# One tile for the first decays, another order of the opening, and two queues for the last stores

## The chip, the cores and the metric

One Trainium2 chip, one core of it. The metric is device time in microseconds (us). Engines are named as in the profile: PE (TensorE, matrix products, with its weight loads PEld), DVE (VectorE), ACT (ScalarE), POOL (GpSimd), SP (SyncE, which issues DMAs). ACT can issue DMAs too; an issue occupies the issuing engine's sequencer, and the transfer then runs by itself. Each engine takes its instructions in the order in which the program was written.

## The reference

Two stages. The first is a scan over a sequence with decays `a`, for 4 sequences, 8 heads, 768 positions; in chunks it reads:

```
log_a = log(clip(a, 1e-6, 1))
cum   = cumsum(log_a in the chunk)
M     = (C @ B.T) * exp(cum_i - cum_j) * (i >= j)
y     = M @ x + (C @ state) * exp(cum)
state = exp(sum log_a) * state + sum_j B_j x_j exp(cum_end - cum_j)
```

Its output, as 3072 tokens of 256 features, goes to the second, a mixture of four experts with gates `p`:

```
p   = probs / (sum(probs) + 1e-9)
out = sum_e p[:, e] * (relu(x @ w1[e]) @ w2[e])
```

All is float32: w1 is 4 x 256 x 1024, w2 4 x 1024 x 256.

## The kernel before

A token chunk is 128 positions; two halves of 64 of every chunk column make a pair p, and 12 pairs cover the sequences. The experts' products run in four blocks of three pairs over 256-wide blocks of features. Sums and differences of weights and of tokens are formed on DVE and POOL so that fewer products are needed (the tables `G` and `B`), and their results are combined on DVE.

The program has two parts. The **opening** (L560 to L786) is written out by hand in the order in which the engines are to take it, and computes the first pair. Everything behind it goes through a **planner** (class `Plan`, L71): every piece of work is added with an engine (or two to choose from), an estimated duration, what it reads and writes, and sometimes a due time. PE's pieces stand in a fixed list `line`; `Plan.run` (L181) walks through a model of time, starting each engine at a time given at the end (`START` for PE, `now` and offsets for the others, L1614), and chooses for the other engines what comes next and which buffer it takes. The order found is the order of the program. Absolute times occur in it as thresholds (`OPENING` 80, `SURE` 100, `BUSY` 200).

What the steps of the prediction touch, in the opening:

- **Loads.** `load_heads` (L445) brings B and C of the four sequences for one chunk column, in two halves of two sequences, both on SP (L569, L579). `load_a` (L573) brings raw decays of one chunk column: 8 KB for each half `s` of the sequences, into every 32nd partition of a tile `a_q[s]` that has been set to zero, one on SP and one on ACT (L577). `a_q2` (L566) are such tiles for the next chunk column, loaded on SP (L589). ACT issues the load of the gates' probabilities first (L570), and two loads of tokens before it loads its table (L582). `load_w1` and `load_w2` follow on SP.
- **Decays.** `ready` (L616) clips a tile on DVE. The clip's upper bound is `own` (L608): 1 in the partitions that hold data, 0 elsewhere. `spread` (L662) sends the decays to the 64 partitions of the half `s` of four banks by a product with ones: first all four row groups `q` for `s` = 0, then for `s` = 1. `scan` (L506) multiplies up the running products from a bank on DVE, one for each `q`.
- **Scores.** `mask` (L486) selects heads of C on ACT; `score` (L492) makes the products C B of one half `s` in four banks `seven`; `masked` (L687) multiplies them by the scans' result on DVE, `aside` (L682) does so for one `q` through ACT and POOL.
- **Gates.** POOL sums the probabilities (L625 to L628), DVE takes the reciprocal (L629), POOL multiplies (L636). `turn_gates` (L644) transposes them on PE into the upper halves of the first two banks `seven[:2]` (called `As`), and ACT copies them out. `spread_gate` (L654) sends them to all partitions through a bank of `seven[2:]` (called `ys`), and ACT copies that.
- **Logs.** `turn_logs` (L700) takes logarithms on ACT, transposes them on PE through a bank (before: `ys[0]`) and ACT copies them; `sum_logs` (L706) makes the sums, which go to DRAM for the later pairs.
- `inner` (L529, products at L532) multiplies the masked scores by the tokens. `idle` (L691) is a product of ones whose result nobody reads; it keeps PE occupied.

PE's order before is at L740 to L782: idle products, `spread`, idle, first half of the scores, turns of the gates, second half of the scores, turns of the logs, spread of the gate, `inner`, the second spread, sums of the logs, the state, the third spread; then the planned `line` with products at L987 (function `product`).

The **end** is `last` (L1378): the results of the last block are turned by PE, copied from their bank by ACT or DVE in turns (L1409, L1461) and stored by `send` (L1395). It is called seven times and issues two DMAs each time, one for each half of the partitions, both on SP.

Of the kernel before, what the change touches and what calls it, by code (L numbers as in the profile page):

```python
# [8 lines left out]
FP32 = mybir.dt.float32  # L9
AF = mybir.ActivationFunctionType  # L10
ALU = mybir.AluOpType

P = 128
# [346 lines left out]
def kernel(  # L360
# [83 lines left out]

    def load_heads(k, bct, zs=slice(0, NSEQ)):  # L445
        src = xbc.rearrange("(z k) r w -> k r z w", k=NC)
        nc.sync.dma_start(out=bct[:, zs], in_=src[k][:, zs, OBT:])

# [43 lines left out]
    def score(p, ctm, bct, banks, half=0, only=None):  # L492
        e = p % 2
        for c in range(2):
            lo = FB * half + P * c
            for s in range(2) if only is None else (only,):
                for r in range(NQ):
                    k, to = slice(32 * r, 32 * r + 32), slice(HALF * s, HALF * s + HALF)
                    nc.tensor.matmul(  # L499
                        out=banks[r][to, lo:lo + P].rearrange("p (t i) -> p t i", t=NT),  # L500
                        lhsT=bct[k, 2 * s + c, 0, HALF * e:HALF * e + HALF],
                        rhs=ctm[k, :, 2 * s + c],
                        start=(c == 0 and not half), stop=True, tile_position=(32 * r, HALF * s),
                        skip_group_check=True)
# [54 lines left out]

    a_q = [homes["V"][-1 - s].rearrange("p c (t x) -> p c t x", t=NT) for s in range(2)]  # L560

# [3 lines left out]
    xt, bct = homes["xt"], homes["bct"]  # L565
    a_q2 = [homes["V"][-4 - s].rearrange("p c (t x) -> p c t x", t=NT) for s in range(2)]  # L566
    nc.vector.memset(a_q[0], 0.0)
    nc.gpsimd.memset(a_q[1], 0.0)
    load_heads(0, bct[0], slice(0, 2))  # L569
    nc.scalar.dma_start(out=pr, in_=probs)  # L570
    a_rows = a.rearrange("(s c k) (q t) x -> k s q c (t x)", s=2, c=2, t=NT)

    def load_a(k, s, a_q, queue):  # L573
        queue.dma_start(
            out=a_q[s].rearrange("(q r) c t x -> q r c (t x)", q=NQ)[:, 0], in_=a_rows[k, s])
# [33 lines left out]
    nc.vector.reduce_sum(  # L609
        own.unsqueeze(2), ident.rearrange("p (q r) -> p r q", r=32)[:, 0:1],  # L610
        axis=mybir.AxisListType.X)

    def clip(engine, v, top=1.0):
        engine.tensor_scalar(out=v, in0=v, scalar1=1e-6, scalar2=top, op0=ALU.max, op1=ALU.min)

    def ready(v, e):  # L616
        v = v.rearrange("p c t (e i) -> p (c t) e i", e=2)[:, :, e]
        clip(nc.vector, v, own)
        nc.vector.memset(v[:, :, 0:1], 0.0)

    for s in range(2):
        ready(a_q[s], 0)

# [4 lines left out]
    nc.gpsimd.tensor_scalar_add(total_p, total_p, 1e-9)  # L628
    nc.vector.reciprocal(total_p, total_p)  # L629
    upto = const.tile([P, P], FP32)  # L630
# [4 lines left out]
    nc.gpsimd.memset(upto[:HALF, HALF:], 0.0)  # L635
    nc.gpsimd.tensor_mul(  # L636
        pc.rearrange("p z e k -> p z k e"), pr.rearrange("p (z k) e -> p z k e", z=NSEQ),
        total_p.rearrange("p (z k) e -> p z k e", z=NSEQ).to_broadcast([P, NSEQ, NC, E]))

    BANK = homes["bank"]  # L640
# [21 lines left out]
    def spread(a_q, e, banks, half, order=range(NQ)):  # L662
        for s in range(2):
            for q in order:
                k = slice(32 * q, 32 * q + 32)
                nc.tensor.matmul(  # L666
                    out=banks[q][HALF * s:HALF * s + HALF, FB * half:FB * half + FB].rearrange(
                        "p (x i) -> p x i", x=4),
                    lhsT=one[k].to_broadcast([32, HALF]),
                    rhs=a_q[s].rearrange("p c t x -> p (c t) x")[k, :, HALF * e:HALF * e + HALF],  # L670
                    start=True, stop=True, tile_position=(32 * q, HALF * s), skip_group_check=True)
# [19 lines left out]
    def idle(bank, lo, to):  # L691
        nc.tensor.matmul(
            out=bank.rearrange("p (w s) -> p w s", s=P)[:, lo:to], lhsT=one.to_broadcast([P, P]),
            rhs=one.unsqueeze(1).to_broadcast([P, to - lo, P]), start=True, stop=True,
            skip_group_check=True)
# [44 lines left out]
    idle(BANK[6], 0, 4)  # L740
    idle(BANK[7], 0, 3)
    spread(a_q, 0, four, 0, ORDER)
    idle(BANK[7], 0, 1)
    for s in range(2):
        mask(0, ctm[0], bct[0], slice(2 * s, 2 * s + 2))
    score(0, ctm[0], bct[0], seven, 0, 0)
    for q in ORDER:
        scan(0, q, MT[0], four[q], 0)
    turn_gates(As)
    score(0, ctm[0], bct[0], seven, 0, 1)  # L750
    clip(nc.gpsimd, a_sb)
# [7 lines left out]
    for s in range(2):  # L759
        ready(a_q[s], 1)  # L760
    for c in range(2):
# [13 lines left out]
    for s in range(2):  # L775
        ready(a_q2[s], 0)
    spread(a_q, 1, four, 1, ORDER)
# [14 lines left out]
    B512, B256 = {"DVE": D512, "POOL": 1.3}, {"DVE": D256, "POOL": .72}  # L792
    now, START = 10.2, 11.6

# [5 lines left out]
    def dma(fn, n=1, kb=256, **kw):  # L800
        return plan.add({"SP": ISSUE * n}, fn, lag=LANDING + kb / 190, kb=kb, pieces=n, **kw)
# [576 lines left out]
    def last(k, groups):  # L1378
# [16 lines left out]
        def send(d, n, r, to):  # L1395
            dma(lambda e: [nc.sync.dma_start(
                out=dst[d, 3 * k + n, c][:, to],
                in_=r.t[HALF * c:HALF * c + HALF, 0, to.start * P:to.stop * P].rearrange(
                    "p (s m) -> p s m", m=P)) for c in range(2)],
                2, kb=64 * (to.stop - to.start), reads=[r])  # L1400

# [269 lines left out]
```

## Time and profile before

| | us |
|---|---|
| median of 3 runs | 617.71 |
| lowest, highest | 615.79, 618.04 |
| the profiled execution | 618.47 |
| its span, first to last instruction | 616.8 |
| granted clock of PE over the span | 0.995 |

| engine | busy us | share of the span |
|---|---|---|
| PE | 603.9 | 98% |
| PEld | 517.8 | 84% |
| DVE | 497.9 | 81% |
| ACT | 276.9 | 45% |
| POOL | 139.3 | 23% |

The profile is of one execution; its times count from the start of the span. A row of its timeline gives the start and the duration in us (of several instructions of one kind together, from the first to the last), the engine, the line of the kernel, the operation, what it writes and reads by the names of the tiles, the shapes, and how many. In brackets stands how long the engine had been idle before, and what ended that. A queue (SPq, ACTq) shows the issuing of DMAs, not their transfer. Matrix products are pipelined, so that rows of PE overlap.

### The profile page before, as it was taken

How to read it: one execution, taken by the hardware profiler on the slowest of the kernel's cores; microseconds unless marked ns; L12 is line 12 of the kernel's file. 1: busy time of each engine (PE TensorE's matmuls, PEld its weight loads, DVE VectorE, ACT ScalarE, POOL GpSimd, SP SyncE). 2: the span in 40 equal slices, each digit the busy share in tenths (PEclk: the TensorE clock that was granted, in tenths of full speed). 3: DMA queues.
4: the chain of work that ended last, by engine and by line, in shares of the span. 5: the costliest groups of instructions: out<-in, count | busy, mean ns of one | idle time of the engine just before them, and what ended most of it. 6: DMA issues, size and time to landing. Idle time of an engine off the chain costs nothing.

```text
span 616.8 us, 12247 instructions
## 1 busy us (share of the span) xinstructions
PE 603.9 (98%) x4526; PEld 517.8 (84%) x4526; DVE 497.9 (81%) x858; ACT 276.9 (45%) x624; POOL 139.3 (23%) x147
## 2 busy tenths in 40 slices
PE   7999999999999999999999999999999999999995
PEld 4777888888888888888888888878888888888884
DVE  4769999999999995786988987486876989485783
ACT  3337557575442626765243343434444242524430
POOL 5572555655610000367401000000000000000000
PEclk9999999999999999999999999999999999999999
DMA  7477677778733329773432416863342323963002
GB/s 206 127 212 211 206 215 244 238 229 292 236 98 113 84 34 324 202 255 137 136 95 69 118 31 172 288 188 95 86 128 70 103 63 62 356 209 94 1 0 53
DMA packets 99856, 93.78 MB, mean 152 GB/s; under 512 B 33500, under 2 KB 69052, under 8 KB 99796
## 3 DMA queue, kind: packets, MB, share of 16 engines
q1 hardware_dynamic: 99272, 92.70, 49.3%
q8 instruction: 36, 0.59, 0.4%
q10 hardware_dynamic: 524, 0.30, 0.2%
q14 instruction: 24, 0.20, 0.1%
HBM read 72.79 MB, written 20.17 MB: 151 GB/s over the span
## 4 chain that ended last, share of the span: by engine, by line
PE 95%; DVE 2%; issue 1%; DMA 1%; ACT 0%; SPq 0%; DVEq 0%
PE bank L987 89%; PE bank L532 2%; PE bank L499 1%; PE bank L920 1%; PE bank L541 1%; DVE v L1022 1%; PE bank L666 1%; DVE MT L520 1%; DMA pr<-in_probs_dram 0%; DVE v L1014 0%; PE bank L1456 0%; DVE bank L1145 0%; PE bank L1393 0%; DVE v L1536 0%; DMA v<-in_a_dram 0%
## 5 line engine op out<-in xcount | busy, mean ns | idle before, releaser
L987 PE MATMUL bank<-v,w 128*128 128x256 f32 x1876 | 435.2, 380 | 1.2 <-DVE bank L1145 0.7
L987 PEld LDWEIGHTS bank<-v,w 128*128 128x128 f32 x1876 | 354.7, 190 | 52.3 <-DVE bank L1145 1.6
L1014 DVE TENSOR_TENSOR v<-v,v 128x512 f32<-128x512 f32 x238 | 177.1, 766 | 1.7
L987 PE MATMUL bank<-Y,w 128*128 128x256 f32 x692 | 177.1, 380 | 0.0
L1287 ACT COPY v<-bank 128x512 f32<-128x512 f32 x120 | 70.3, 586 | 202.7 <-PE bank L987 199.1
L987 PEld LDWEIGHTS bank<-Y,w 128*128 128x128 f32 x692 | 130.6, 190 | 19.4 <-ACT v L996 0.9
L1022 DVE SCALAR_TENSOR_TENSOR v<-bank,gate 128x512 f32<-128x512 f32 x162 | 111.1, 686 | 40.2 <-PE bank L987 35.5
L1047 POOL TENSOR_TENSOR w<-w,w 128x512 f32<-128x512 f32 (+1 forms) x84 | 94.1, 1132 | 104.6 <-DVE v L1022 32.7
L1001 ACT COPY bank<-v 128x512 f32<-128x512 f32 x141 | 81.7, 593 | 20.7 <-DVE v L1022 14.5
L1145 DVE TENSOR_TENSOR bank<-bank,v 128x512 f32<-128x512 f32 x92 | 62.6, 693 | 33.7 <-PE bank L987 23.3
L996 ACT COPY v<-bank 128x512 f32<-128x512 f32 x111 | 65.1, 587 | 53.0 <-PE bank L987 45.3
L515 ACT ACTIVATE MT<-ab,neg 128x64 f32<-128x64 f32 x144 | 37.4, 338 | 0.0
L1014 DVE TENSOR_TENSOR v<-bank,v 128x512 f32<-128x512 f32 x30 | 20.6, 685 | 9.3 <-PE bank L987 6.4
L1323 DVE TENSOR_TENSOR v<-v,v 128x256 f32<-128x256 f32 x65 | 24.5, 416 | 1.0 <-ACT v L1287 0.7
L1022 DVE SCALAR_TENSOR_TENSOR v<-v,gate 128x512 f32<-128x512 f32 x30 | 24.1, 804 | 0.4
L882 POOL TENSOR_TENSOR cts<-ctm,dec 128x512 f32<-128x512 f32 x11 | 14.0, 1270 | 36.0 <-DVE Y L1117 24.2
L939 ACT COPY v<-bank 64x256 f32<-64x256 f32 (+1 forms) x33 | 12.3, 373 | 19.6 <-PE bank L541 12.4
L1014 POOL TENSOR_TENSOR v<-v,v 128x512 f32<-128x512 f32 x12 | 15.2, 1271 | 16.0 <-DVE v L1014 9.7
L689 DVE TENSOR_TENSOR MT<-bank,MT 128x256 f32<-128x256 f32 x47 | 16.6, 412 | 1.6 <-PE bank L499 1.6
L520 DVE TENSOR_TENSOR MT<-MT,bound 128x512 f32<-128x512 f32 x18 | 15.8, 891 | 0.0
L489 ACT ACTIVATE ctm<-bct,tmask 128x256 f32<-128x256 f32 (+1 forms) x26 | 11.4, 485 | 7.0 <-DMA bct<-in_xbc_dram 6.9
L532 PEld LDWEIGHTS bank<-MT,xt 64*32 64x32 f32 x768 | 10.1, 109 | 2.9 <-issue 2.0
(95 smaller groups left out, 188.7 us busy)
## 6 DMA issues: line engine op xcount, KB each, us to landing
w<-w_d SPq DMA_DIRECT2D x128, 256.0 KB
w<-in_w_dram SPq DMA_DIRECT2D x72, 256.0 KB
w_d<-w SPq DMA_DIRECT2D x64, 256.0 KB
gate<-p_d SPq DMA_DIRECT2D x15, 384.0 KB
ab<-cum_d SPq DMA_DIRECT2D x36, 128.0 KB
xt<-in_xbc_dram SPq DMA_DIRECT2D x46, 96.0 KB
bct<-in_xbc_dram SPq DMA_DIRECT2D x5, 512.0 KB
out_dram<-v SPq DMA_DIRECT2D x144, 16.0 KB
```

Source lines behind the costliest of these rows:

```text
L515: nc.scalar.activation(out=MT[:, q, c, t], in_=ab[:, c, h], func=AF.Exp, bias=neg[:, e, t, i:i + 1])
L520: nc.vector.tensor_tensor(out=v, in0=v, in1=bound.unsqueeze(1).to_broadcast([P, 4 * n, HALF]), op=ALU.min)
L532: nc.tensor.matmul(out=y[to:to + 32], lhsT=xt[k, c, h:h + D], rhs=MT[k, q, c, t], start=start, stop=True, tile_position=(HALF * s, to), sk ...
L987: nc.tensor.matmul(out=o, lhsT=w[:, j], rhs=x if half is None else x[:, j], start=(start and j == 0), stop=(j == 1), skip_group_check=True)
L996: act(.5, lambda e: nc.scalar.copy(out=flat(v), in_=bank.t), reads=[bank], writes=[v])
L1001: act(.54 if to - lo > FB else .32, lambda e: nc.scalar.copy(out=bank.t[:, lo:to], in_=flat(v)[:, lo:to]), reads=[v], writes=[bank])
L1014: plan.add(engines, lambda e: (on(e).tensor_add if sign > 0 else on(e).tensor_sub)(flat(v), whole(x), whole(y)), reads=[x, y], writes=[v], ...
L1022: dve(D512, lambda e: nc.vector.scalar_tensor_tensor(out=h.t, in0=whole(x).rearrange("p (j m) -> p j m", j=JJ), scalar=0.0, in1=g.t[:, 2 * ...
L1047: (on(e).tensor_add if sign > 0 else on(e).tensor_sub)(out, x, y)
L1145: dve(D512, lambda e: (nc.vector.tensor_add if sign > 0 else nc.vector.tensor_sub)(to.t, bank.t, whole(x)), reads=[x, bank], writes=[to])
L1287: act(.5, lambda e: nc.scalar.copy(out=flat(v), in_=bank.t), reads=[bank], writes=[v], hold=HOLD)
L1323: plan.add(engines, lambda e: (on(e).tensor_add if sign > 0 else on(e).tensor_sub)(o[1](), x[1](), y[1]()), reads=[v for v in vs if v is n ...
```

## The change

- The tiles `a_q[0]` and `a_q[1]` become one tile, `a_q`, with the half `s` in every 32nd partition counted from `s`; so do those of `a_q2`. `ready` clips the whole tile in one instruction with an upper bound of 1. `own` now has two columns, a mask of the rows of each half, and takes the place of the ones in `spread`, which goes through the halves inside each row group.
- The loads of the decays come before the heads; the second half of the heads is issued by ACT. Two w1 loads come before those of `a_q2`.
- The reciprocal and the multiplication of the gates move behind the first scan; the gates are turned before both halves of the scores, which follow each other. The logs are turned behind `inner`, through `As[1]`. One idle product is cut from 384 to 256 columns, one of 128 is added before the masks, one of 128 ahead of `inner`.
- The planner's `now` and `START` become 0.6 smaller, and two tiles of V fewer are marked as used by the opening.
- `send` puts its two DMAs into the plan one by one, the first on SP, the second on ACT.

```diff
-    def load_heads(k, bct, zs=slice(0, NSEQ)):
+    def load_heads(k, bct, zs=slice(0, NSEQ), queue=nc.sync):
...
-    a_q = [homes["V"][-1 - s].rearrange("p c (t x) -> p c t x", t=NT) for s in range(2)]
+    a_q, a_q2 = (homes["V"][-i].rearrange("p c (t x) -> p c t x", t=NT) for i in (1, 4))
...
-    nc.vector.memset(a_q[0], 0.0)
-    nc.gpsimd.memset(a_q[1], 0.0)
-    load_heads(0, bct[0], slice(0, 2))
+    nc.vector.memset(a_q[:, 0], 0.0)
+    nc.gpsimd.memset(a_q[:, 1], 0.0)
     nc.scalar.dma_start(out=pr, in_=probs)
...
-            out=a_q[s].rearrange("(q r) c t x -> q r c (t x)", q=NQ)[:, 0], in_=a_rows[k, s])
+            out=a_q.rearrange("(q r) c t x -> q r c (t x)", q=NQ)[:, s], in_=a_rows[k, s])
 
     for s, queue in enumerate((nc.sync, nc.scalar)):
         load_a(0, s, a_q, queue)
-    load_heads(0, bct[0], slice(2, 4))
+    load_heads(0, bct[0], slice(0, 2))
+    load_heads(0, bct[0], slice(2, 4), nc.scalar)
...
-    for s in range(2):
-        nc.vector.memset(a_q2[s], 0.0)
+    nc.vector.memset(a_q2, 0.0)
+    for fb in range(2):
+        load_w1(fb, homes["W"][fb])
     for s in range(2):
         load_a(1, s, a_q2, nc.sync)
-    for fb in range(4):
+    for fb in range(2, 4):
...
-    own = const.tile([P, 1], FP32)
+    own = const.tile([P, 2, 1], FP32)
...
-        clip(nc.vector, v, own)
+        clip(nc.vector, v)
...
-        for s in range(2):
-            for q in order:
+        for q in order:
+            for s in range(2):
...
-                    lhsT=one[k].to_broadcast([32, HALF]),
+                    lhsT=own[k, s].to_broadcast([32, HALF]),
...
-    idle(BANK[7], 0, 3)
+    idle(BANK[7], 0, 2)
     spread(a_q, 0, four, 0, ORDER)
+    idle(BANK[7], 0, 1)
     idle(BANK[7], 0, 1)
     for s in range(2):
         mask(0, ctm[0], bct[0], slice(2 * s, 2 * s + 2))
-    score(0, ctm[0], bct[0], seven, 0, 0)
-    for q in ORDER:
+    for i, q in enumerate(ORDER):
         scan(0, q, MT[0], four[q], 0)
+        if not i:
+            nc.vector.reciprocal(total_p, total_p)
+    nc.gpsimd.tensor_mul(
+        pc.rearrange("p z e k -> p z k e"), pr.rearrange("p (z k) e -> p z k e", z=NSEQ),
...
     turn_gates(As)
-    score(0, ctm[0], bct[0], seven, 0, 1)
+    for s in range(2):
+        score(0, ctm[0], bct[0], seven, 0, s)
...
-    turn_logs(ys[0])
     spread_gate(ys[1], homes["gate"][0])
-    for s in range(2):
-        ready(a_q[s], 1)
+    idle(four[0], 2, 3)
+    ready(a_q, 1)
...
+    turn_logs(As[1])
     for s, copy in enumerate((nc.scalar.copy, nc.vector.tensor_copy)):
...
-    now, START = 10.2, 11.6
+    now, START = 9.6, 11.0
...
-    for i in (0, NV - 5, NV - 4, NV - 2, NV - 1):
+    for i in (0, NV - 4, NV - 1):
...
         def send(d, n, r, to):
-            dma(lambda e: [nc.sync.dma_start(
-                out=dst[d, 3 * k + n, c][:, to],
...
-                2, kb=64 * (to.stop - to.start), reads=[r])
+            for c, (queue, on_) in enumerate(((nc.sync, "SP"), (nc.scalar, "ACT"))):
+                plan.add({on_: ISSUE}, lambda e, c=c, queue=queue: queue.dma_start(
...
+                        "p (s m) -> p s m", m=P)), lag=LANDING + .2, kb=32 * (to.stop - to.start),
+                    reads=[r])
```

More of the change, by code (lines that the diff above doesn't have):

```diff
@@ L443, in load_tokens @@
                 out=xt[HALF * s:HALF * s + HALF, c], in_=src[s, c, k, e][:, :OBT])
-    def load_heads(k, bct, zs=slice(0, NSEQ)):
+    def load_heads(k, bct, zs=slice(0, NSEQ), queue=nc.sync):
         src = xbc.rearrange("(z k) r w -> k r z w", k=NC)
-        nc.sync.dma_start(out=bct[:, zs], in_=src[k][:, zs, OBT:])
+        queue.dma_start(out=bct[:, zs], in_=src[k][:, zs, OBT:])
     def load_decays(p, ab):
@@ L607, with clip @@
                             op0=ALU.mult, op1=ALU.add)
-    own = const.tile([P, 1], FP32)
+    own = const.tile([P, 2, 1], FP32)
     nc.vector.reduce_sum(
[L610 to L614, printed above, removed]
+        own, ident.rearrange("p (q r) -> p r q", r=32)[:, 0:2], axis=mybir.AxisListType.X)
+    def clip(engine, v):
+        engine.tensor_scalar(out=v, in0=v, scalar1=1e-6, scalar2=1.0, op0=ALU.max, op1=ALU.min)
     def ready(v, e):
         v = v.rearrange("p c t (e i) -> p (c t) e i", e=2)[:, :, e]
-        clip(nc.vector, v, own)
+        clip(nc.vector, v)
         nc.vector.memset(v[:, :, 0:1], 0.0)
-    for s in range(2):
-        ready(a_q[s], 0)
+    ready(a_q, 0)
     pairs = const.tile([P, T // P, 2], FP32)
@@ L774 @@
              in_=ys[s][:, :FB].rearrange("p (c t i) -> p c t i", c=2, t=NT))
-    for s in range(2):
-        ready(a_q2[s], 0)
+    ready(a_q2, 0)
     spread(a_q, 1, four, 1, ORDER)
```

13 lines of the change are left out of this document (4 added, 9 removed).

## The prediction, made before the result was known

> **What bounds the kernel now.** First the page's chain by engine and the busy time of each engine over the planned middle, then the two ends in order of time.
>
> ```profile
> PE 95%; DVE 2%; issue 1%; DMA 1%; ACT 0%; SPq 0%; DVEq 0%
> ```
> ```profile
> 20.00:600.00 580.00, 578.76 (x4269) 500.77 (x4269) 483.62 (x812) 270.08 (x607) 129.99 (x119) 1.00 0.50 154
> 46.00:231.00 185.00, 184.48 (x1500) 158.36 (x1499) 180.86 (x298) 102.38 (x264) 73.06 (x63) 1.00 0.59 184
> ```
>
> The columns of the second fence are the stretch, its length, and the busy time of PE, PEld, DVE, ACT and POOL. The chain is PE's, and from 20 to 600 us PE is busy 578.76 of 580: it can win at most 1.2 us there. So the change can gain only ahead of the first weight product and behind the last matmul. In 46 to 231 us DVE is at 180.86 of 185 too; this is where the middle could lose.
>
> The opening in order of time (start, busy, instruction, what ended the idle time before it), on PE, then DVE, ACT, POOL and SP's queue:
>
> ```profile
> 0.84 3.33 PE L692 MATMUL bank<-const-float32-1.0 128*128 128x512 f32 x4 [0.84 <-PEq L1663]
> 6.11 1.57 PE L666 MATMUL bank<-v,const-float32-1.0 32*64 32x256 f32 x16 [1.94 <-DVE v L619]
> ...
> 8.33 1.13 PE L499 MATMUL bank<-ctm,bct 32*64 32x128 f32 x16
> 9.39 1.03 PE L646 MATMUL bank<-ident,pc 128*24 128x128 f32 x4
> 10.44 1.08 PE L499 MATMUL bank<-ctm,bct 32*64 32x128 f32 x16
> 12.31 0.39 PE L703 MATMUL bank<-ident,cum 96*128 96x96 f32 x2 [0.78 <-ACT cum L701]
> 12.62 0.69 PE L655 MATMUL bank<-v,ident 24*128 24x256 f32 x2
> ...
> 13.78 2.33 PE L532 MATMUL bank<-MT,xt 64*32 64x64 f32 x62 [0.24 <-ACT gate L659]
> 16.03 1.16 PE L666 MATMUL bank<-v,const-float32-1.0 32*64 32x256 f32 x16
> ...
> 19.94 2.43 PE L987 MATMUL bank<-v,w 128*128 128x256 f32 x10
> ```
> ```profile
> 5.57 0.75 DVE L614 TENSOR_SCALAR v<-v,own 128x256 f32<-128x256 f32 x2 [2.45 <-DMA v<-in_a_dram]
> ...
> 6.36 0.29 DVE L629 RECIPROCAL total_p<-total_p 128x24 f32<-128x24 f32 x1
> ...
> 7.66 2.44 DVE L507 TENSOR_TENSOR_SCAN MT<-bank,identr 128x256 f32<-128x256 f32 x4 [1.01 <-PE bank L666]
> 11.68 1.09 DVE L689 TENSOR_TENSOR MT<-bank,MT 128x256 f32<-128x256 f32 x3 [1.58 <-PE bank L499]
> ```
> ```profile
> 1.36 1.16 ACTq L574 DMA_DIRECT2D v<-in_a_dram  x1
> 2.55 1.17 ACTq L442 DMA_DIRECT2D xt<-in_xbc_dram  x2
> 3.74 1.28 ACT L582 ACT_TABLE_LOAD   x1 [3.74 <-issue]
> 5.04 0.69 ACT L489 ACTIVATE ctm<-bct,tmask 128x128 f32<-128x128 f32 x2
> 6.68 0.69 ACT L489 ACTIVATE ctm<-bct,tmask 128x128 f32<-128x128 f32 x2 [0.95 <-DMA bct<-in_xbc_dram]
> 10.03 0.79 ACT L650 COPY v<-bank 24x256 f32<-24x256 f32 x2 [2.66 <-PE bank L646]
> ```
> ```profile
> 3.76 0.26 POOL L625 TENSOR_TENSOR pairs<-pr 128x48 f32<-128x48 f32 x1 [1.12 <-DMA pr<-in_probs_dram]
> ...
> 6.74 0.36 POOL L636 TENSOR_TENSOR pc<-pr,total_p 128x96 f32<-128x96 f32 x1 [1.22 <-DVE total_p L629]
> ```
> ```profile
> 0.80 0.44 SPq L447 DMA_DIRECT2D bct<-in_xbc_dram  x1
> 1.49 0.74 SPq L574 DMA_DIRECT2D v<-in_a_dram  x1
> 2.28 0.52 SPq L447 DMA_DIRECT2D bct<-in_xbc_dram  x1
> ```
>
> The reader is to see one chain. The decays land behind half of the heads; DVE clips them at 5.57; PE spreads them from 6.11; scores, turns of the gates and scores follow each other to 11.52; the products of L532 start at 13.78 and the first weight product at 19.94.
>
> The end, on ACT, DVE and SP's queue (the last two rows from two windows):
>
> ```profile
> 607.09 0.37 ACT L1409 COPY v<-bank 128x256 f32<-128x256 f32 x1 [3.52 <-PE bank L1393]
> 608.43 0.27 ACT L1461 COPY v<-bank 128x128 f32<-128x128 f32 x1 [0.98 <-PE bank L1456]
> 608.65 0.37 ACT L1409 COPY v<-bank 128x256 f32<-128x256 f32 x1
> ```
> ```profile
> 608.06 0.42 DVE L1409 COPY v<-bank 128x256 f32<-128x256 f32 x1 [0.64 <-PE bank L1393]
> 609.55 0.29 DVE L1461 COPY v<-bank 128x128 f32<-128x128 f32 x1 [1.07 <-PE bank L1456]
> ```
> ```profile
> 603.59 10.96 SPq L1396 DMA_DIRECT2D out_dram<-v  x14
> ```
> ```profile
> 612.04 2.51 SPq L1396 DMA_DIRECT2D out_dram<-v  x4
> ```
>
> All results are in SBUF at 609.55 + 0.29 = 609.84, yet SP issues until 603.59 + 10.96 = 614.55, at 2.51/4 = 0.63 us each; the span closes 2.25 later, at 616.8. So 4.7 us behind the last copy go to a queue of issues.
>
> **Last stores on two queues: 2.9 us less.** Seven sends give two DMAs each; after, SP and ACT issue seven each. The first two sends lie in ACT's 3.52 us of idle time, so its wait there for DVE's result holds up nothing. Five issues a queue are left. SP: one at 607.5, when the third result is copied, then from 608.5 (608.06 + 0.42) four back to back, to 608.5 + 4 x 0.63 = 611.0. On ACT stand besides the copies of 608.43 and 608.65, which end at 609.02; they are all that waits behind an issue there, with the stores of what they copy. Four issues after 609.02 end near 611.6. Last issue 614.55 to 611.6: 2.9 us. Bounds: 3.5 if the copies cost ACT nothing; 0.9 if each of its issues takes the 1.16 us of the row at 1.36 (609.02 + 4 x 1.16 = 613.7). I stay near 0.63: the two ACT issues at 2.55 took 1.17 together while SP issued beside them.
>
> **First decays: the clip 2 us earlier.** One tile takes the place of two, and both loads wait for both memsets, now of half the size. SP issues near 1.25 with nothing ahead, ACT behind its probabilities. No row shows such a landing. The nearest, the probabilities, first on their queue as well, were issued at about 0.8 and used at 3.76: 2.95 us, so 4.2 at the latest. The last store closed 2.25 us behind its issue, everything after it included; with half of that, 1.25 + 0.6 + 1.1 = 3.0 at the earliest. I take 3.6. From clip to spread is 6.11 - 5.57 = 0.54: PE at 4.1. The idle products, seven units of 128 columns in 3.33 us and now six, end at 4.17 - 0.48 = 3.7. The spread with all operands there takes 1.16 (row 16.03) instead of 1.57, and bank by bank, so scans start at 5.2; four (2.44) and the reciprocal put between them (0.29) end at 7.9 instead of 10.1.
>
> **Heads and masks: nothing.** The second half goes to ACT, behind its load, near 2.5, where SP issued it at 2.28; the first half goes behind SP's load. The same bytes move, so I leave the last mask ending at 6.68 + 0.69 = 7.4, a us either way. The table load slides by one issue to end near 5.5, under the transfer of the heads.
>
> **Turns ahead of both scores: 1.3 us.** Reciprocal at 5.8, gates on POOL (0.36) to 6.6, turns (1.03) to 7.6. ACT's two copies of them (0.79) stand behind the masks: 7.4 to 8.2. Both scores write the banks that these copies read; the second score of before began as they went (10.44 against 10.03), so I let the scores wait: from 7.8 on, 1.13 + 1.08 end near 10.2 (9.4 if the column halves overlap, 11.2 with late masks) instead of 11.52. Scans that end at 7.9 are out of the chain.
>
> **Logs behind the products: 0.1 us.** From 11.52 to 13.78 are 2.26 us, with 0.78 of waiting for the logarithm. After: the first masking with its hand-over 0.5 (1.09/3 + 0.14), the gate's spread 0.69, its copy 0.37 as at 608.65, and hand-overs 0.2: 1.8. The new idle product lies in the time of that copy; without that cover it costs its 0.48 (the unit above). Turning the logs later gives 0.39 back on PE; ACT's copy of them lies beside the next spread's 1.16.
>
> So L532 starts near 12.0 and the opening gives 1.4, say **1.5** with some overlap of the scores; bounds 0.2 (landing 4.2, masks late) and 2.7 (landing 3.0, scores overlapped, masks early).
>
> **At nothing:** the wider reduce, done while the load flies; fewer V tiles to be freed; w1 ahead of the second decays, which only the third spread needs. START shifts all planned times by 0.6, and DVE, ACT, POOL and SP may be ordered otherwise: the middle, which can win 1.2 us, I put at 0, from -0.6 to +1.5.
>
> The clock:
>
> ```profile
> 14.00:16.00 2.00, 2.00 (x62) 1.86 (x58) 0.00 (x0) 0.00 (x0) 1.93 (x4) 0.50 1.02 319
> ```
>
> The clock granted was 0.50 in this stretch, that of L532. At full speed its 2.33 us would be about half. I keep it slow; a shifted phase is worth up to 1.1 us.
>
> **The sum.** 1.5 + 2.9 = 4.4. The profiled execution took 618.47 (span 616.8), 0.76 above the median of 617.71: it would come to 614.1, the median to **613.3**.
>
> **Rivals.** *The second queue helps little* (0.10): an issue from ACT costs 1.16, or the two halves are served in turn. For: the row at 1.36. Against: that at 2.55. Stores 0.9, sum 2.4: 615.3.
>
> The Trainium skill, "DMA: Bandwidth & Descriptors", Rules for kernel authors, says of two transfers to disjoint partition halves not to bother, as they share the same engines and serialize. By that rule the stores give nothing and the time is 616.2; the row at 612.04 speaks against it here, as it is issuing that is queued.
>
> *The decays come no earlier* (0.13): both loads now write interleaved rows of one tile. If the second waits for the first to land, ACT's heads and masks stand 2 us longer and the clip is back near 5.5. Against: the halves of the heads, one tile too, were issued at 0.80 and 2.28, the second long before 6.68. Opening 0: 614.8. *The middle absorbs the opening* (0.05): PE comes earlier, DVE, full from 46 to 231, doesn't: 614.8. Against: its planned scans hang on the same spreads. *Slower* (0.04): the new order moves sums from POOL to DVE in that stretch.
>
> ```profile
> L1014 DVE TENSOR_TENSOR v<-v,v 128x512 f32<-128x512 f32 x238 | 177.1, 766 | 1.7
> ...
> L1047 POOL TENSOR_TENSOR w<-w,w 128x512 f32<-128x512 f32 (+1 forms) x84 | 94.1, 1132 | 104.6 <-DVE v L1022 32.7
> ```
>
> DVE has 185 - 180.86 = 4.1 us free there and pays 0.77 for a sum of 512 columns (766 ns). Five of POOL's 84 fill it; each further one can stall PE by 0.77, and from 5 + 4.4/0.77 = 11 the kernel is slower. Eighteen cost 18 x 0.77 - 4.1 = 9.8 us: 623.
>
> **Numbers.** Forecast 0.68, by itself 611.5 to 615.0. With the rivals 611.0 to 616.0. About 0.5%, 3.1 us, is what a measurement of this kernel can tell from no change. Below 614.6 lies most of the forecast and a little of the rivals: faster 0.73, same 0.23, slower 0.04.
>
> **What would show it.** Stores: issues on both queues, the last ending near 611.6; wrong if ACT's take 1.2 or a copy stands long behind one. Decays: clip near 3.6, scans from 5.2; wrong if the clip stays past 5. Scores: ending near 10.2, waiting for ACT's copies; wrong if masks end past 8.4. Middle: first weight product to last copy stays 609.55 - 19.94 = 589.6; wrong past 591.

## The result and the profile after

| | us | runs |
|---|---|---|
| after, median (lowest to highest) | 614.44 (613.46 to 615.61) | 8 |
| before, beside it | 617.39 (615.79 to 618.36) | 8 |
| ratio, 95% interval | 0.9954 (0.9939 to 0.9970) | |
| the profiled execution of after | 613.47 | |
| its span; mean granted clock | 611.7; 0.997 | |

The change makes the kernel 2.95 us faster, where 4.4 was forecast. The two profiled executions lie 5.0 us apart (618.47 and 613.47): before's is one of its longer executions, after's nearly its shortest. So the profiles show where the time comes from, but not how much of it.

The opening of after on PE (start, busy, instruction, what ended the idle time before):

```profile
4.09 0.69 PE L659 MATMUL bank<-v,own 32*64 32x256 f32 x16 [0.35 <-POOL upto L628]
...
6.23 0.61 PE L639 MATMUL bank<-ident,pc 128*24 128x128 f32 x4 [0.81 <-POOL pc L744]
7.29 0.98 PE L499 MATMUL bank<-ctm,bct 32*64 32x128 f32 x32 [0.45 <-ACT v L643]
10.29 0.78 PE L648 MATMUL bank<-v,ident 24*128 24x256 f32 x2 [2.01 <-DVE MT L682]
...
11.72 2.39 PE L532 MATMUL bank<-MT,xt 64*32 64x64 f32 x64
...
17.74 4.58 PE L985 MATMUL bank<-v,w 128*128 128x256 f32 x20
```

The first weight product starts at 17.74, where before had 19.94. Up to the scores everything came as forecast or earlier: they end at 7.29 + 0.98 = 8.27. But then PE stands idle for 2.01 us, a wait that before did not have. The same stretch on DVE, then on POOL:

```profile
3.57 0.29 DVE L613 TENSOR_SCALAR v<-v 128x256 f32<-128x256 f32 x1 [1.25 <-DMA v<-in_a_dram]
...
4.85 0.69 DVE L507 TENSOR_TENSOR_SCAN MT<-bank,identr 128x256 f32<-128x256 f32 x1 [0.85 <-PE bank L659]
...
5.65 1.79 DVE L507 TENSOR_TENSOR_SCAN MT<-bank,identr 128x256 f32<-128x256 f32 x3
9.81 1.09 DVE L682 TENSOR_TENSOR MT<-bank,MT 128x256 f32<-128x256 f32 x3 [2.37 <-POOL ends L673]
```
```profile
8.33 1.07 POOL L613 TENSOR_SCALAR cum<-cum 96x256 f32<-96x256 f32 x1 [2.15 <-DMA cum<-in_a_dram]
9.46 0.56 POOL L673 COPY ends<-MT 128x4 f32<-128x4 f32 x4
```

DVE's masking (L682) could start when the scores are there, at 8.3, and starts at 9.81. It overwrites the tile MT in place, and the last column of each scan must first be copied out of it into `ends` by POOL (L673). POOL has these copies behind its clip of `a_sb` (L613, the tile `cum`), and that clip waits until 8.33 for the load of `a_sb`. The scans have been done since 7.44.

The end, on ACT, on DVE and on SP's queue:

```profile
606.41 0.71 ACTq L1395 DMA_DIRECT2D out_dram<-v  x1
607.16 0.37 ACT L1408 COPY v<-bank 128x256 f32<-128x256 f32 x1 [0.56 <-issue]
607.24 1.94 ACTq L1395 DMA_DIRECT2D out_dram<-v  x3
```
```profile
607.44 0.29 DVE L1460 COPY v<-bank 128x128 f32<-128x128 f32 x1 [1.07 <-PE bank L1455]
```
```profile
601.48 7.99 SPq L1395 DMA_DIRECT2D out_dram<-v  x7
```

The last copy ends at 607.44 + 0.29 = 607.73. SP issues until 609.47, ACT until 609.18, and the span closes at 611.7. Behind the last copy lie 4.0 us, where before had 616.8 - 609.84 = 7.0: the stores gave 3.0. Between the first weight product and the start of the last copy lie 607.44 - 17.74 = 589.70 us, where before had 589.61: as a sum, the middle gave nothing and took nothing. Within it PE now waits once, for 0.82 us ahead of 40.59, where before has PE idle nowhere from 20 to 46 us; from 46 to 231 us PE is idle for 0.46 less.

### The profile page after: what moved, and what is told of

It reads as the page before. It is cut to its first block, busy times and chain, and to the rows that moved or that the text cites. A ratio compares the mean times of both kernels' runs of the same rounds, so it can differ in the third digit from the quotient of the medians.

```text
span 611.7 us, 12256 instructions
## 1 busy us (share of the span) xinstructions
PE 600.8 (98%) x4530; PEld 516.8 (84%) x4530; DVE 493.8 (81%) x851; ACT 276.6 (45%) x624; POOL 140.4 (23%) x147
## 4 chain that ended last, share of the span: by engine, by line
PE 97%; DMA 1%; issue 0%; SPq 0%; DVE 0%; POOL 0%; ACT 0%; DVEq 0%; POOLq 0%
PE bank L985 91%; PE bank L532 2%; PE bank L499 1%; PE bank L918 1%; DMA cum<-in_a_dram 1%; PE bank L541 1%; PE bank L1455 0%; PE bank L1391 0%; PE bank L659 0%; SPq L442 0%; PE bank L648 0%; PE bank L685 0%; DVE bank L1143 0%; DVE v L1020 0%; SPq L447 0%
## 5 line engine op out<-in xcount | busy, mean ns | idle before, releaser
L1012 DVE TENSOR_TENSOR v<-v,v 128x512 f32<-128x512 f32 x238 | 175.1, 757 | 1.7
L1045 POOL TENSOR_TENSOR w<-w,w 128x512 f32<-128x512 f32 (+1 forms) x84 | 95.6, 1151 | 102.9 <-DVE v L1012 31.1
L682 DVE TENSOR_TENSOR MT<-bank,MT 128x256 f32<-128x256 f32 x47 | 16.6, 411 | 2.4 <-POOL ends L673 2.4
L532 PEld LDWEIGHTS bank<-MT,xt 64*32 64x32 f32 x768 | 9.8, 110 | 2.4 <-issue 2.0
```

Of the source, the lines that this page charges most:

```text
L532: nc.tensor.matmul(out=y[to:to + 32], lhsT=xt[k, c, h:h + D], rhs=MT[k, q, c, t], start=start, stop=True, tile_position=(HALF * s, to), sk ...
L682: nc.vector.tensor_mul(v, bank[:, FB * half:FB * half + FB], v)
L1012: plan.add(engines, lambda e: (on(e).tensor_add if sign > 0 else on(e).tensor_sub)(flat(v), whole(x), whole(y)), reads=[x, y], writes=[v], ...
L1045: (on(e).tensor_add if sign > 0 else on(e).tensor_sub)(out, x, y)
```

## The experiments

Each kernel ran beside the kernel before on the same chip. Three chips were used: the first four kernels of the table ran on one, the next four on a second, the last two on a third. The medians of before there were 617.96, 618.09 and 618.30.

| kernel | median us (lowest to highest) | runs | ratio to before, 95% interval |
|---|---|---|---|
| stores alone | 614.52 (613.01 to 615.80) | 12 | 0.9948 (0.9928 to 0.9969) |
| opening alone | 617.30 (616.42 to 618.68) | 12 | 0.9987 (0.9966 to 1.0008) |
| changed kernel again | 614.64 (613.81 to 618.05) | 12 | 0.9953 (0.9932 to 0.9975) |
| ends first | 612.75 (610.98 to 614.29) | 6 | 0.9912 (0.9878 to 0.9946) |
| ends first, heads first | 616.01 (614.02 to 619.43) | 10 | 0.9970 (0.9942 to 0.9998) |
| ends first, old turns | 614.78 (611.60 to 615.83) | 10 | 0.9931 (0.9899 to 0.9963) |
| ends first, filled | 612.83 (610.99 to 613.30) | 7 | 0.9906 (0.9873 to 0.9939) |
| ends first, no idle | 614.09 (613.50 to 616.71) | 10 | 0.9932 (0.9904 to 0.9960) |
| fills alone | 613.74 (613.22 to 615.10) | 6 | 0.9929 (0.9907 to 0.9951) |
| ends first again | 614.46 (611.27 to 617.37) | 8 | 0.9932 (0.9909 to 0.9955) |

My theory: the stores give about 3 us; of the opening's gain, POOL's new wait eats a part. The rival: the opening's gain depends on the clock that PE is granted, and the two profiles met different phases of it.

**Stores alone, and opening alone.** The kernel before with the new `send`:

```diff
-            dma(lambda e: [nc.sync.dma_start(
...
+            for c, (queue, on_) in enumerate(((nc.sync, "SP"), (nc.scalar, "ACT"))):
+                plan.add({on_: ISSUE}, lambda e, c=c, queue=queue: queue.dma_start(
```

> The kernel before with the send of the changed kernel alone: the two halves of each last store go to SP and ACT. Theory of this study (two separate gains that add up; the stores give what the profiles show): last copy to span end 4.0 us instead of 7.0, first weight product near 19.9 as before, the median 3.0 us below before (614.4). Rival (the medians moved by 2.95 because the opening gave about that and the stores little): median within 1 us of before. The opening is that of before, so the spread between executions should stay some 2.5 us.

And the changed kernel with the old one (the same lines the other way):

> The changed kernel with the send of before: opening and planner shift alone. If the opening is worth the 2.2 us that the two profiles show: first weight product near 17.7, median 2.2 us below before (615.2). Rival (the profiled execution of before was a slow one and that of after a fast one by the phase of PE's clock, and the opening is worth little between typical executions): first weight product 17.7 to 19.5 from execution to execution, median within 0.8 us of before. Last copy to span end 7.0 in both.

The stores alone gain 617.96 - 614.52 = 3.44 us (interval 1.9 to 4.4), all that the whole change gains beside them (3.32). Their end, on ACT, DVE and SP's queue:

```profile
609.70 2.16 ACTq L1397 DMA_DIRECT2D out_dram<-v  x3
```
```profile
609.76 0.29 DVE L1462 COPY v<-bank 128x128 f32<-128x128 f32 x1 [1.07 <-PE bank L1457]
```
```profile
603.80 7.75 SPq L1397 DMA_DIRECT2D out_dram<-v  x7
```

The last copy ends at 610.05, both queues by 611.9, the span at 614.1: 4.0 us again. The opening alone keeps its 14 issues on SP:

```profile
602.68 10.75 SPq L1394 DMA_DIRECT2D out_dram<-v  x14
```

That is until 613.43, with the last copy at 608.92 and the span at 615.6: 6.7 us. Its first weight product starts at 19.00. Its gain of 0.66 us has an interval from 2.1 faster to 0.5 slower, in which both nothing and the forecast 1.5 lie. So the stores are settled, and the question is where the opening's 1.5 went.

**The changed kernel again**, unedited.

> The changed kernel itself, in the same rounds as the others, to have its times and its spread on this chip beside theirs: 2.95 us below before. If the phase of PE's clock in the opening makes the spread, its profile shows a first weight product other than 17.7 whenever the half-clock stretch lies elsewhere than at 10.8 to 14.2.

It came to 614.64, as after, and beside it the stores alone came to 614.52. Resampled, the twelve times of each give a 95% interval for the rest of the change, from 0.7 slower to 0.5 faster: a gain of 1.5 isn't in it. The profile of this run is another opening than the one above, on PE:

```profile
4.24 1.16 PE L659 MATMUL bank<-v,own 32*64 32x256 f32 x16 [0.50 <-POOL upto L629]
...
7.90 1.61 PE L499 MATMUL bank<-ctm,bct 32*64 32x128 f32 x32
10.22 1.22 PE L648 MATMUL bank<-v,ident 24*128 24x256 f32 x2 [0.70 <-DVE MT L682]
...
12.09 2.39 PE L532 MATMUL bank<-MT,xt 64*32 64x64 f32 x64
14.40 0.58 PE L696 MATMUL bank<-ident,cum 96*128 96x96 f32 x2
14.91 1.16 PE L659 MATMUL bank<-v,own 32*64 32x256 f32 x16
16.00 1.17 PE L701 MATMUL bank<-upto,w 128*96 128x128 f32 x4
...
19.21 1.13 PE L985 MATMUL bank<-v,w 128*128 128x256 f32 x4
```

The same 16 products of the spread take 1.16 us here and 0.69 in the profile above; PE runs at half speed until about 17 us. The scores end at 9.51, so POOL's copies are nearly done by then and PE's wait is 0.70, not 2.01. The first weight product starts at 19.21, 1.47 us later than in the other execution of the same program. The profile of the stores alone, whose opening is that of before, happens to have the same clock (16 products of L666 take 1.03 at 16.49, 0.72 at 19.06; its decays landed early, with the spread at 5.33), and so the two can be laid side by side. Neither is typical: 615.80 is the longest of the twelve times of the stores alone, 615.24 the third longest here.

```profile
13.64 2.91 PE L532 MATMUL bank<-MT,xt 64*32 64x64 f32 x64
16.49 1.03 PE L666 MATMUL bank<-v,const-float32-1.0 32*64 32x256 f32 x16
17.45 0.68 PE L708 MATMUL bank<-upto,w 128*96 128x128 f32 x4
...
19.06 0.72 PE L666 MATMUL bank<-v,const-float32-1.0 32*64 32x256 f32 x16
...
20.20 1.99 PE L987 MATMUL bank<-v,w 128*128 128x256 f32 x8
```

At L532 the new opening leads by 13.64 - 12.09 = 1.55 us; at the first weight product by 20.20 - 19.21 = 0.99. What lies between took 6.56 us in the old opening and 7.12 in the new one, but it isn't the same work. The new opening turns the logs there (0.51, from 14.40 to 14.91); in the old one's row of L532 the first two products start half a us before the others, which wait for ACT's copy of the gate until 14.12. From the second spread on the work is the same. There the new opening leads by 16.49 - 14.91 = 1.58, so it loses 0.59 from there to the first weight product. Full speed came at about 17 us in both, and the new opening, being earlier, does more of that work at half speed: the spread takes 1.16 against 1.03, the sums (L701) take 1.17, those of the old (L708) 0.68. At the start of DVE's last copy, at 608.98 in the changed kernel against 609.76, the lead is 0.78, and in the whole time of the two executions (615.24 and 615.80) 0.56.

**Ends first.** The changed kernel with POOL's four copies ahead of its clip, so that they no longer stand behind a load that they don't need:

```diff
-    clip(nc.gpsimd, a_sb)
     for q in ORDER:
         end_of(q)
+    clip(nc.gpsimd, a_sb)
```

> The changed kernel with one swap on POOL: the copies of the decays' ends (L673) come before the clip of the logs' input, not behind it. In the changed kernel the masking (L682) starts at 9.81, 1.5 us behind the scores, because those copies stand on POOL behind a clip that waits for its load until 8.33. Theory (that wait is what binds between scores and products): masking near 8.5, L532 near 10.4 instead of 11.72, first weight product 1.3 us earlier, median 1.0 to 1.4 below the changed kernel. Rival (the product of the third group on POOL or the gate's spread binds next): L532 gains less than 0.5.

> The kernel with the copies of the ends ahead of POOL's clip once more, beside the fills alone and the kernel before on one chip. If its lead is its own and not the other chip's: 612.2 to 613.3, ratio 0.990 to 0.993. If its six runs were lucky ones: 614 to 615, like the changed kernel.

In the first of these two, on PE, on DVE and on POOL:

```profile
7.74 0.98 PE L499 MATMUL bank<-ctm,bct 32*64 32x128 f32 x32 [0.79 <-ACT v L643]
9.43 0.69 PE L648 MATMUL bank<-v,ident 24*128 24x256 f32 x2 [0.70 <-DVE MT L682]
...
10.47 2.26 PE L532 MATMUL bank<-MT,xt 64*32 64x64 f32 x64
...
17.01 3.29 PE L985 MATMUL bank<-v,w 128*128 128x256 f32 x14
```
```profile
8.95 1.09 DVE L682 TENSOR_TENSOR MT<-bank,MT 128x256 f32<-128x256 f32 x3 [1.41 <-PE bank L499]
```
```profile
7.60 0.19 POOL L673 COPY ends<-MT 128x4 f32<-128x4 f32 x1 [0.39 <-DVE MT L507]
8.23 1.07 POOL L613 TENSOR_SCALAR cum<-cum 96x256 f32<-96x256 f32 x1 [0.44 <-DMA cum<-in_a_dram]
```

The masking now follows the scores by 0.23 us (8.72 to 8.95) instead of 1.54, PE waits 0.70 instead of 2.01, and L532 starts at 10.47. In this execution the mechanism is shown. Its worth in medians is not: 612.75 on one chip, 1.9 under the changed kernel beside it, but 614.46 on another, no better than after. The profile of that second set is one with half speed early (its spread takes 1.16, its scores end at 9.53), here on DVE and PE:

```profile
9.76 1.09 DVE L682 TENSOR_TENSOR MT<-bank,MT 128x256 f32<-128x256 f32 x3 [1.69 <-PE bank L499]
```
```profile
12.11 2.39 PE L532 MATMUL bank<-MT,xt 64*32 64x64 f32 x64
```

The changed kernel again, slow early too, had its masking at 9.74 and L532 at 12.09: there the copies' order gave nothing, as the scores end late enough to hide POOL. Half speed early doesn't always hide it. In the profile of the opening alone the load of `a_sb` lets POOL's clip begin only at 8.96; the scores end at 9.45 and the masking starts at 10.44.

The single times point the same way, sorted by the mean granted clock listed with each. At 0.997 (3.41 us of half speed are 0.5 x 3.41/611 = 0.003) four of the five executions with the ends first took 612.74 to 612.86, the fifth 617.37; the six of the changed kernel, both sets together, 613.46 to 614.12. At 1.000 no half speed is recorded, and what is slow ahead of the records isn't counted: the six with the ends first took 614.15 to 615.11, the eight of the changed kernel 614.30 to 615.75. By the medians of these kinds the copies' order is worth 1.1 us (612.80 and 613.90) in the one, and 0.1 (614.51 and 614.64) in the other. Three more with the ends first, at 0.999, took 610.98 to 611.27, and six more of the changed kernel, at other means, 614.61 to 618.05. This sorting was made when the times were known, and the mean says little of the opening itself. In the profiles with 0.998 and 0.999 the half speed that is recorded lies behind the last product (in the changed kernel again from about 611 us on), and the profile of the old turns, at 0.997, starts slowly (its spread takes 1.16). So it is a hint and no proof.

**Old load order, old turns.** Two parts of the change undone, one at a time, in the kernel with the ends first. The heads ahead of the decays again:

```diff
+    load_heads(0, bct[0], slice(0, 2))
     nc.scalar.dma_start(out=pr, in_=probs)
...
-    load_heads(0, bct[0], slice(0, 2))
-    load_heads(0, bct[0], slice(2, 4), nc.scalar)
+    load_heads(0, bct[0], slice(2, 4))
```

> The kernel of e3 with the loads of before: half of the heads ahead of the decays on SP, the other half on SP too. Theory (the decays' place in the queue is what made the opening earlier): clip at 4.7 to 5.6 instead of 3.63, as in the two profiles of the old order, scans, reciprocal and turns as much later, scores ending near 10 instead of 8.7, first weight product 0.8 to 1.3 us later than e3's at the same clock, median 0.5 to 1.5 above e3 (613.3 to 614.3). Rival (masks or POOL bind anyway): first weight product within 0.3 of e3's, median the same.

PE's order of before, with a half of the scores on either side of the turns:

```diff
+    score(0, ctm[0], bct[0], seven, 0, 0)
     for i, q in enumerate(ORDER):
...
-    for s in range(2):
-        score(0, ctm[0], bct[0], seven, 0, s)
+    score(0, ctm[0], bct[0], seven, 0, 1)
```

> The kernel of e3 with the old order on PE: first half of the scores, turns of the gates, second half of the scores. Theory (the order of turns and scores is worth little; what my forecast put down to it, 1.3 us, came from the earlier decays): scores end within 0.4 us of e3's 8.72 at the same clock, median within 0.5 of e3. Rival (the order is worth its 1.3 us): scores end near 10, first weight product 1.3 later.

With the heads first the clip starts at 4.75, as expected, the spread at 5.28 and L532 at 13.12. The profile, one of the two longest of the ten executions, has half speed even in the first weight products:

```profile
5.28 1.16 PE L659 MATMUL bank<-v,own 32*64 32x256 f32 x16 [1.54 <-DVE v L618]
...
13.12 2.39 PE L532 MATMUL bank<-MT,xt 64*32 64x64 f32 x64
...
21.30 1.22 PE L985 MATMUL bank<-v,w 128*128 128x256 f32 x2
```

The median is 616.01, 1.7 above the range that was expected, and more than the stores alone (614.52, on another chip; the intervals of the ratios overlap): without the early decays no gain can be measured of the rest of the new opening. The old turns gave two groups of times: 611.60, 611.72, 611.85 and 611.96 at a mean clock of 0.999, and 615.38, 615.41, 615.72 and 615.83 at 1.000, besides one each of 614.17 and 615.45. One program, 3.8 us apart. The list shows only that the mean clocks differ, by 0.001, and the profile is of neither group (614.17; scores ending at 9.89, first weight product at 18.12), so what parts them isn't shown. The median moves with how many executions fall on each side, and whether the turns ahead of both scores gain anything isn't settled by it.

**Idle products.** If the clock decides, products of ones in PE's waits should steady it. Five more of them, of 128 columns, with the ends first, and then with POOL's order as the change has it:

```diff
-    idle(BANK[7], 0, 1)
-    idle(BANK[7], 0, 1)
+    for _ in range(3):
+        idle(BANK[7], 0, 1)
...
     turn_gates(As)
+    for _ in range(2):
+        idle(BANK[7], 0, 1)
     for s in range(2):
         score(0, ctm[0], bct[0], seven, 0, s)
+    for _ in range(2):
+        idle(four[0], 2, 3)
```

> The kernel of e3 with five more idle products of 128 columns in PE's waits: one more behind the first spread, two behind the turns, two behind the scores. Theory (the clock granted in the first 17 us follows how busy PE was in the window of 3.4 us before, and the waits cost half clock): no stretch of half clock at 10.9 to 14.4, L532 in 1.2 us instead of 2.3, first weight product near 15.9 instead of 17.0, median 0.5 to 1.2 below e3 and less spread. Rival (the filling doesn't change the clock, and at half clock it outlasts the waits): first weight product up to 1 us later, median above e3.

> The changed kernel with five more idle products of 128 columns in TensorE's waits of the opening, and POOL's clip left ahead of the copies of the ends, where the change has it. If the wait on POOL's clip costs the time by itself, the full clock that the fills bring makes the scores end near 9, the first masking stays past 9.7, and the kernel is 1 to 2 us above the one with the ends first. If the wait mattered only because TensorE stood idle in it and lost the clock, the fills take its place: within 0.5 us of the one with the ends first, and the products of L532 at full speed, near 1.5 us.

And none at all in the opening (it leaves out the idle products, whose results nobody reads):

> The kernel of e3 without any idle product in the opening. Theory of the clock: PE stays at half clock until the products of L532 have filled a window, full clock from 14 to 17.5 us, first weight product 18 to 19.2 as in the slow executions of the changed kernel, median 1 to 2 us above e3 (613.8 to 614.8). Rival (idle products do nothing for the clock): first weight product at 17.0 or earlier, median the same or lower.

On PE, the filled kernel with the ends first, then the fills alone, then the one without idle products:

```profile
11.23 1.52 PE L532 MATMUL bank<-MT,xt 64*32 64x64 f32 x64
...
16.33 3.94 PE L989 MATMUL bank<-v,w 128*128 128x256 f32 x17
```
```profile
11.68 1.53 PE L532 MATMUL bank<-MT,xt 64*32 64x64 f32 x64
...
16.79 7.17 PE L989 MATMUL bank<-v,w 128*128 128x256 f32 x32
```
```profile
11.43 2.91 PE L532 MATMUL bank<-MT,xt 64*32 64x64 f32 x64
...
18.69 1.56 PE L980 MATMUL bank<-v,w 128*128 128x256 f32 x6
```

With the fills L532 takes 1.52 and 1.53 us, and the first weight product starts 5.1 us after it, where the changed kernel's two profiles have 6.0 and 7.1. Without idle products L532 takes 2.91, of which half a us is the wait of all but its first two products for the gate; it then runs at half speed, as in the changed kernel. The times of these two kernels, both with the ends first and on one chip, agree: all seven of the filled one (610.99 to 613.30) lie under all ten of the one without idle products (613.50 to 616.71), by 1.26 us in the medians. Against the ends first, on other chips, the filled median is level with the first set (612.75) and 1.6 under the second (614.46), where 0.5 to 1.2 under was expected. The idle products that the change has gain nothing by themselves that these runs show: without any, the ratio is 0.9932, as with the ends first again.

The fills alone, on one chip with the ends first again, came out 0.7 under it (613.74 and 614.46). The ranges overlap, and by resampling the difference may be anything from 1.5 under to 1.1 above. They are not 1 to 2 us above, although the first masking is still late (10.16). But it isn't shown either that the new wait costs time by the clock that is lost in it: the ends first, whose PE waited only 0.70 there, ran L532 at half speed all the same (2.26). And between the two filled profiles POOL's order still makes 0.46 us at the first weight product (16.33 and 16.79).

Not all of the lead arrives at the end. In the filled kernel the last copy starts at 607.22 (DVE), so the middle took 607.22 - 16.33 = 590.89, 1.2 more than after's 589.70. PE's busy time (the first number behind the comma) in 20 to 600 us, of after and of the filled kernel:

```profile
20.00:600.00 580.00, 578.39 (x4268) 500.51 (x4267) 480.52 (x810) 268.60 (x602) 131.43 (x119) 1.00 0.50 154
```
```profile
20.00:600.00 580.00, 577.81 (x4263) 499.78 (x4262) 481.14 (x807) 268.59 (x602) 129.74 (x118) 1.00 0.51 154
```

PE is idle 0.6 us more there: 0.39 ahead of 34.85 and 1.02 ahead of 39.28, where after has the 0.82 ahead of 40.59. The profiles show nothing that PE waits for at these places, so the cause stays open. That the middle can't follow so early a start isn't shown: ends first again starts its first weight product at 18.80 and has such a wait of 1.08, with a middle of 590.20, while the kernel without idle products starts it at 18.69, has none, and a middle of 589.07.

The filled one with the ends first has the lowest ratio, 0.9906 (0.9873 to 0.9939), at 612.83 us. It is under before, and its interval hardly overlaps those of the changed kernel (0.9939 to 0.9970 and 0.9932 to 0.9975). From the ends first (0.9912) and the fills alone (0.9929) it can't be told apart.

## Why the prediction was right in one term and wrong in another

- **Last stores: right.** Forecast 2.9, measured 3.0 by the profiles and 3.4 by the medians. The last issue was to end 611.6 - 609.84 = 1.76 behind the last copy, and ends 609.47 - 607.73 = 1.74 behind it. ACT's last three issues took 0.65 each, near the 0.63 taken from SP's row and far from the 1.16 of the other bound (0.72 in the stores alone and in the changed kernel again, where one more took 1.09); the copy at 607.16 stood behind an issue for 0.56, as foreseen. The Trainium skill, "DMA: Bandwidth & Descriptors", Rules for kernel authors, has two transfers to disjoint partition halves serialize whichever engine issues them, and advises against the split. No run here shows whether these transfers did. The advice doesn't hold for this end of a kernel: a queue of 14 issues was the bound, and two queues took 3.0 us off it.
- **First decays: right in their times, not in what they were compared with.** Clip at 3.57 (forecast 3.6), spread at 4.09 (4.1), scans from 4.85 to 7.44 (5.2 to 7.9). The second load did not wait for the first: SP issued its load at 1.29 and ACT at 1.32, and the clip, which needs both, starts at 3.57. But the clip of before at 5.57, against which the 2 us were counted, was a late one. In the two other profiles with the old order of the loads it starts at 4.76 (stores alone) and 4.75 (heads first), which leaves 1.2.
- **Heads and masks, turns: right in their order, too late in their size.** The scores wait for ACT's copies of the gates, as said, but end at 8.27 (9.51 in the second profile) and not at 10.2: the masks of both halves ran together from 5.59 to 6.99, and the two halves of the scores took 0.98 or 1.61, not 2.21.
- **Logs behind the products: wrong by a wait that was not on the list.** From the scores to the gate's spread I had 0.5 us, one masking with its hand-over; it took 2.0 in the first profile and 0.7 in the second. The row was there in before, on POOL:

```profile
8.14 1.07 POOL L614 TENSOR_SCALAR cum<-cum 96x256 f32<-96x256 f32 x1 [1.04 <-DMA cum<-in_a_dram]
...
10.16 0.19 POOL L680 COPY ends<-MT 128x4 f32<-128x4 f32 x1 [0.40 <-DVE MT L507]
```

A clip that begins at 8.14, takes 1.07 and has four copies behind it sets a floor of about 9.8 for the masking, by an estimate from these rows. Before, the scans hid it (the last copy waited for one until 10.16), and with the scores at 10.2 as forecast it would have stayed hidden. That the two errors cancelled was luck: L532 starts at 11.72 and 12.09 in the two profiles, forecast 12.0.
- **The opening's 1.5: the term that failed.** Its lead at L532 is there (1.55 in the pair with full speed at about 17 us). But from the lead at L532 the sum took off only the 0.39 for the logs, and carried the rest unchanged to the end of the kernel. In that pair it is 1.58 at the second spread, shrinks to 0.99 at the first weight product and is 0.56 in the whole time, and over all executions nothing can be measured of it: 614.64 for the whole change, 614.52 for the stores alone. The term was also sized on one profile of before, whose clip came 0.8 later than in the two others of that order; how often it does, no run shows.
- **The clock: the step behind that.** "I keep it slow; a shifted phase is worth up to 1.1 us" took the phase for an uncertainty of one product group. It is more: the same program starts its first weight product at 17.74 or 19.21. That the lead shrinks because full speed does not come earlier when the work does is shown for one pair of profiles, and there for 0.6 us of it. Why a typical execution of the change gains nothing over the stores alone stays open.
- **Middle: right as a sum**, 589.70 against 589.6, though with a wait of 0.82 in it that before didn't have. The rival in which the middle absorbs the opening was given 0.05. It doesn't hold for the change by this sum. In the filled kernel part of the lead is lost in the middle (590.89), but that DVE is what holds PE up, as the rival had it, isn't shown.
- **The sum.** 4.4 was forecast between medians and 2.95 measured; the 1.45 that lack are about the size of the opening's term. The time fell inside the stated range because the larger term, the stores, was right.

## What to carry to other kernels

Behind the last result count the issues that are still queued, and split them over engines that have nothing left to do: that term was worked out to a tenth of a microsecond from one row. Size a term on more than one profile of before: here one execution's late load made the opening's gain look larger. Where a chain is shortened, look in each engine's order for what stands ahead of the next step's operands (here a clip behind a load) and work out when it would be done; a hidden wait shows as soon as the chain is faster than it. A lead in a part that runs before PE's full clock is not yet a lead at the end; take several executions before a profile's opening is believed.

## What the runs showed of the hardware

PE's clock in the opening of after, in three stretches (length; PE, PEld, DVE, ACT, POOL busy; the granted clock is the third number from the right):

```profile
7.36:10.77 3.41, 1.40 (x34) 0.89 (x34) 1.04 (x4) 0.52 (x2) 2.38 (x7) 1.00 0.99 285
10.77:14.18 3.41, 3.41 (x68) 2.79 (x68) 0.51 (x3) 0.69 (x2) 2.99 (x7) 0.50 0.90 265
14.18:17.59 3.41, 2.86 (x78) 1.70 (x78) 0.95 (x4) 0.96 (x3) 0.00 (x0) 1.00 0.65 198
```

Full speed, then half for 3.41 us, then full again. The half follows a stretch in which PE was busy for only 1.40 us, 41%, and the stretch in which it was busy throughout is followed by full speed. The busy share alone doesn't decide, though. With the ends first, half speed, again for 3.42 us, follows at 10.94 a stretch with 2.49 us, 73%:

```profile
7.53:10.94 3.41, 2.49 (x54) 1.72 (x57) 1.38 (x6) 1.48 (x5) 2.81 (x6) 1.00 0.87 267
```

and in after full speed went on at 7.36 behind a stretch from 3.95 with 2.01 us, 59%.

The Trainium skill, "TensorE: Matmul & The Clock Gate", Part 1, "What's actually happening", describes a monitor that judges PE by windows of about 3.4 us which run freely and don't start with the kernel; length and order agree here, and so does that one program meets different phases (0.69 and 1.16 for the same 16 products at 4.1 and 4.2). The Trainium skill, in the same section, calls the cost under 1% of a typical span. It is: 19.21 - 17.74 = 1.47 us of 614 are 0.2%. But that is as large as the whole term that was forecast for the opening. One thing doesn't agree. The same section of the Trainium skill has full speed behind the first busy 3.4 us or so. In the second profile of the changed kernel PE is busy from 10.22 to 17.17 without idle time, 6.95 us or two such windows, and at half speed all through it (the rows from L648 to L701 above). How busy a stretch must be, or with what products, to be followed by full speed isn't settled by these runs.

A caution in reading: the clock column shows 1.00 ahead of the first change that the trace recorded. In the second profile of the changed kernel it says 1.00 for a stretch in which the spread took 1.16 us and the turns 1.03, half speed by the 0.69 and 0.61 of the other execution. There the durations tell the clock, not the column.
